# Stage borders of a gated attention and memory kernel: clears, stores and sweep steps issued elsewhere, a gate gradient as a column of other products

## The chip, the cores and the metric

The kernel runs on one core of one Trainium2 chip. The metric is the device time of one execution in microseconds (us), given as the median of several runs. TensorE (PE) does the matrix products, VectorE (DVE), ScalarE (ACT) and GpSimd (POOL) do the elementwise work, and SyncE (SP) issues transfers. SP, ACT and POOL each have a queue from which they issue DMAs. Each engine carries out its own instructions in the order of the program; what passes between engines is kept in order by semaphores.

## The reference

The reference computes a gated mix of two token mixers on the same input `x` (2048 tokens of 576), and the gradients of everything for a given `grad_out`:

```python
g = sigmoid((x * gate_w).sum(-1, keepdims=True))
a = A(x, A_wq, A_wk, A_wv, A_wo)      # 32 query heads of 18, one shared k and v, softmax over all 2048 keys
b = B(x, mem0, Wq, Wk, Wv, Wo, 32)    # 64 segments of 32 tokens, one after the other
out = g * a + (1 - g) * b
# B, for each segment: h = [mem (8 rows); segment (32 rows)], 32 heads of 128,
#   masked softmax attention within h, o = attention @ Wo, mem = o[:8], output rows = o[8:]
# returned: out, and the gradients of x, A_wq, A_wk, A_wv, A_wo, mem0, Wq, Wk, Wv, Wo, gate_w
```

In B the memory of a segment comes out of the segment before it, so its forward and its backward pass are chains of 64 steps. All tensors are bfloat16.

## The kernel before

The kernel is a sequence of stages, and each stage has its own tiles. Names of tiles carry a prefix by stage.

- **Preparation and projections** (0 to about 470 us).
- **Forward weave** (to 2123 us): the 64-step chain of B (`b_chain_fwd`, tiles `c_...`) woven with the first pass of A over blocks of 512 queries and 4 heads (`a_pass1`, tiles `a_...`). A block ends with `a_post`: the accumulator is copied to `a_acs` by ACT, transposed by PE (`c_x`), copied to `a_tk` by ACT, and POOL works out `a_ot`, `a_t`, `a_dq` and `a_qc`, which are stored by DMA to `otok_dram`, `dqtok_dram` and `qs_dram`. In the chain's last segment POOL also issues the stores of `c_oT`, `c_vmT`, `c_oh` and `memT_hist`, and makes `c_oh` from `c_oT` by a copy.
- **Bulk** (`b_bulk`, 2127 to 2762 us, tiles `x_...`): attention within segments for all tokens, 128 ticks in 32 chunks of four. Each tick goes through a written list of stages: transposes of q and dO (`x_tr`, copied to `x_qT` by DVE), scores, an exponential on ACT (`x_E`), a normalization on POOL (`x_P`), and so on. The memory rows of k and v lie in four tiles `x_kmB`, `x_vmB` (two each) that are cleared once and then have only their diagonal blocks loaded. SP loads chunks ahead in the order of `load(...)` calls.
- **Sweep and lead** (2763 to 2851 us): `a_pass2` is the second pass of A, a generator of sweep steps. One step is a score product (`b_S`), an exponential on ACT (`b_E`, 128x1024), the product `b_dP`, a product with the exponentials on DVE (`b_dS`) and accumulations (`b_acc`). A step reads a block of `qs_dram` (`b_QS`). `lead_dw` computes the gradients of two weights in units of 16 products into the PSUM tiles `r_pj` and `r_x` in turn; a unit's result is copied to `r_kvo` by ACT and stored by POOL. The generator yields after every 11 products.
- **Backward weave** (to 4369 us): the 64-step backward chain (`b_chain_bwd`, tiles `r_...`) woven with sweep steps. Its weights `WT` (12 pieces of 1152 KB) are loaded by SP, at points of the lead that `early_bwd` lists.
- **`b_post`** (to 4583 us, tiles `y_...`).
- **`b_dw`** (4583 to 5345 us): the gradients of the weights of B and `out`. For k = 0 to 15 the token rows of two blocks of 512 columns (`w_d`, 2 MB each, loaded one k ahead) are multiplied with the tokens (`w_h`) in groups; a group of k < 4 is two runs of 20 products of 128x288, the first 16 over tokens and the last 4 over memory rows. Sweep steps are issued between products, one whenever `WCOLS` columns have been computed. After the groups of each k, `gate` computes 128 rows of `out`: 10 products, then a chain on DVE (`o_diff`, `o_out`, `o_dg`, the gate's gradient `dz_all`).
- **`a_final`** (5345 to 5404 us, tiles `f_...`): transposes of `wq` into `f_wqT`, and for each of 16 token tiles five transposes (`f_ptr`), their copy (`f_T`), twelve products into `f_big`, a DVE step and a POOL step to `f_dx` and its store. Between them 80 small products `f_pk` give the gradients of wk and wv, `f_k`.

Products of all stages go through one helper, so PE's lines in the profile are L87 (products) and L92 (transposes), and evacuations by ACT and DVE are often L84 and L82. Stages up to `b_dw` are issued in the order in which the program writes them; in `a_final` a scheduler chooses the order.

Of the kernel before, what the change touches and what calls it, by code (L numbers as in the profile page):

```python
# [16 lines left out]
P = 128  # L17
# [23 lines left out]
WCOLS = 13824  # L41
# [10 lines left out]
class Kern:  # L52
# [295 lines left out]
    def b_chain_fwd(self, keep, sp, psum):  # L348
# [71 lines left out]
        for s in range(NSEG):  # L420
# [21 lines left out]
            def mT_store(w):  # L442
                nc.gpsimd.dma_start(self.mTd[w][s], mT[w][:].rearrange("p c u t -> p (c u) t"))
# [113 lines left out]
            nc.gpsimd.dma_start(self.oTm_dram[s // 16][:, s % 16, :], oT[:].rearrange("p u c q -> p (u c q)"))  # L557
# [10 lines left out]
            if s % 4 == 3:  # L568
                c0 = 8 * (s % 16 - 3)
                nc.gpsimd.dma_start(self.oh_dram[s // 16][:, :, c0:c0 + 32], oh[:].rearrange("p c u t -> p (c u) t"))  # L570
# [11 lines left out]
            else:  # L582
                nc.gpsimd.dma_start(self.memT_dram[:], hist[:])
# [87 lines left out]
    def early_bwd(self, i):  # L671
# [11 lines left out]
        for k in range(4):  # L683
# [4 lines left out]
            if i == PRE + 32 + k:  # L688
                self.load_WT(8 + k)

    def lead_dw(self, kvp, psum):
        nc = self.nc
        units = [(self.WT[w], o, kt, hf) for w, o in ((0, 2), (1, 5)) for kt in range(NKT) for hf in range(2)]
        n, out = 0, None
        for u, (t, o, kt, hf) in enumerate(units):
            rows = KT_ROWS[kt]
            pw = psum.tile([P, 512], F32, name=("r_pj", "r_x")[u % 2], bufs=1)
            for tt in range(self.NTT):
# [9 lines left out]
            def out(pw=pw, o=o, kt=kt, hf=hf, rows=rows):  # L708
                o16 = kvp.tile([P, 4, P], BF16, name="r_kvo", bufs=2)
                f = o16[0:rows].rearrange("p a b -> p (a b)")[:, 0:288]  # L710
                nc.scalar.copy(f, pw[0:rows, 0:288])
                nc.gpsimd.dma_start(self.outs[o][kt * P:kt * P + rows, 288 * hf:288 * hf + 288], f)
        out()
# [12 lines left out]
    def b_bulk(self, wp, lp, sp, psum):  # L726
# [4 lines left out]
        for t in mB["v"] + mB["k"]:  # L731
            nc.vector.memset(t[:], 0.0)
# [263 lines left out]
        for names in (deep, ("v", "vB", "kB")):  # L996
            load(1, names)
# [3 lines left out]
        for t in range(NG + 9):  # L1001
            for n, st in order:
# [445 lines left out]
    def b_dw(self, sp, wA, wB, wH, psum, sweep):  # L1448
# [30 lines left out]
        def groups(k, ts, ht):  # L1479
            if k < 4:  # L1480
                od = self.outs[10].rearrange("h e d -> (h e) d")
                for t, cs in ts:
                    for i in range(4):
                        o16 = sp.tile([P, D], BF16, name="w_o16b", bufs=3)
                        for hf in range(2):
                            acc = psum.tile([P, 512], F32, name="w_acc", bufs=3)
                            for it in range(n):
                                self.mm(acc[:, 0:288], lhsT=t[:, it, 128 * i:128 * i + 128],
                                        rhs=ht[:, it, 288 * hf:288 * hf + 288], start=(it == 0), stop=(it == n - 1))
                                weave(288)  # L1490
                            self.evac(o16[:, 288 * hf:288 * hf + 288], acc[:, 0:288])
# [27 lines left out]
        with self.tc.manual_schedule():  # L1519
# [7 lines left out]
            for _ in range(6):  # L1527
                next(sweep)
            for k in range(16):
# [13 lines left out]
                for _ in groups(k, ts, ht):  # L1543
# [4 lines left out]
            dz16 = sp.tile([P, NTT], BF16, name="w_dz", bufs=1)  # L1548
            nc.vector.tensor_copy(dz16[:], self.dz_all[:])
            pg = [psum.tile([P, 512], F32, name="w_acc", bufs=3) for _ in range(2)]  # L1550
            for tt in range(NTT):
                for hf in range(2):
                    self.mm(pg[hf][0:1, 0:288], lhsT=dz16[:, tt:tt + 1], rhs=ht[:, tt, 288 * hf:288 * hf + 288],
                            start=(tt == 0), stop=(tt == NTT - 1))
            dg16 = sp.tile([P, 2, 288], BF16, name="w_dg", bufs=1)
            for hf in range(2):
                nc.vector.tensor_copy(dg16[0:1, hf, :], pg[hf][0:1, 0:288])
            nc.sync.dma_start(self.outs[11][None, :], dg16[0:1].rearrange("p a b -> p (a b)"))
# [692 lines left out]
```

## Time and profile before

| | |
|---|---|
| median of 3 runs | 5409.53 us (5405.29, 5409.53, 5409.9) |
| profiled execution | 5406.08 us, of it span 5404.4 us |
| mean granted PE clock | 0.984 |
| busy: DVE, ACT, POOL | 66%, 61%, 41% of the span |
| DMA | 959.71 MB, mean 178 GB/s |

All views that are shown come from that one profiled execution. In a timeline, a row gives the start, the busy time, engine, line, operation, output and inputs and the number of instructions, and in brackets the engine's idle time before it and what ended it. A row of waits gives what an engine waited for: us in total, times, the longest. A row of stretches gives the busy time of PE, PE's weight load, DVE, ACT and POOL (instructions in brackets), the granted PE clock, the share of the DMA engines that is busy and GB/s.

### The profile page before, as it was taken

The numbers are of one execution on the slowest core, as the hardware profiler recorded it, in microseconds if no ns is written. First come the engines' busy times: TensorE is split into PE (matmuls) and PEld (weight loads), VectorE is DVE, ScalarE is ACT, GpSimd is POOL, SyncE is SP. The second block draws the span as 40 slices with busy tenths as digits, with TensorE's granted clock in tenths as the row PEclk, the third lists the DMA queues.
The fourth block names the chain that finished last, engine by engine and source line by source line (L and its number), as shares of the span: only waits on it lengthen the run. The fifth ranks groups of instructions, "written<-read, shape, count | busy, mean of one in ns | idle before, by whom it ended". The sixth has DMA issues, their size and how long they took to land. (4 is left out here: it accounts for less than half of the span.)

```text
span 5404.4 us, 221739 instructions
## 1 busy us (share of the span) xinstructions
PE 5156.3 (95%) x95713; PEld 2791.6 (52%) x95713; DVE 3568.7 (66%) x7079; ACT 3307.3 (61%) x4753; POOL 2189.9 (41%) x4199
## 2 busy tenths in 40 slices
PE   8999999999999998999988999999999999999998
PEld 6434444444444444666654555555555567754444
DVE  5337888888888887666657777878888841333322
ACT  4326778878888886555556777777777732222211
POOL 4004556565565655333323444444444421111213
PEclk9999999999999999999999999999999999999999
DMA  6645666676666555788885677888888778966653
GB/s 217 223 172 136 136 136 137 136 142 141 140 139 127 118 110 148 239 250 250 257 272 173 164 180 175 180 180 183 180 181 176 166 191 209 270 207 201 199 166 93
DMA packets 1065785, 959.71 MB, mean 178 GB/s; under 512 B 617506, under 2 KB 920363, under 8 KB 1054818
## 3 DMA queue, kind: packets, MB, share of 16 engines
q1 hardware_dynamic: 953762, 687.59, 52.8%
q0 software_dynamic: 102752, 248.05, 14.8%
q8 instruction: 749, 12.27, 1.0%
q10 hardware_dynamic: 8288, 9.87, 0.6%
q14 instruction: 234, 1.92, 0.1%
HBM read 518.41 MB, written 375.52 MB: 165 GB/s over the span
## 5 line engine op out<-in xcount | busy, mean ns | idle before, releaser
L1990 DVE TENSOR_TENSOR b_dS<-b_dP,b_E 128x512 bf16<-128x512 f32 x2048 | 1317.7, 685 | 584.6 <-PE b_dP L87 262.1
L1825 DVE TENSOR_TENSOR a_W<-a_dP,a_E 128x512 bf16<-128x512 f32 x2048 | 1314.5, 684 | 238.4 <-issue 108.5
L1939 ACT ACTIVATE b_E<-b_S 128x1024 bf16<-128x1024 f32 x1024 | 1049.5, 1025 | 626.8 <-PE b_dP L87 540.9
L1795 ACT ACTIVATE a_E<-a_S 128x1024 bf16<-128x1024 f32 x1024 | 1050.0, 1025 | 251.7 <-PE a_dP L87 166.9
L87 PE MATMUL r_pj<-WT,r_dT 128*32 128x288 bf16 x12288 | 488.9, 289 | 8.6 <-DMA WT<-st_WT 4.8
L87 PE MATMUL w_acc<-w_d,w_h 128*128 128x512 bf16 (+1 forms) x2400 | 484.1, 379 | 0.0
L87 PEld LDWEIGHTS <-b_QS 32*128 32x128 bf16 (+1 forms) x8192 | 229.2, 90 | 429.5 <-issue 376.8
L87 PE MATMUL b_S<-b_KV,b_QS 32*128 32x512 bf16 x2048 | 404.0, 387 | 36.7 <-ACT b_E L1939 24.5
L87 PE MATMUL a_S<-a_QD,l_KV 32*128 32x512 bf16 x2048 | 399.5, 384 | 38.4 <-ACT a_E L1795 36.1
L87 PE MATMUL a_acc<-a_W,l_WK 128*32 128x512 bf16 x4096 | 413.9, 390 | 1.3 <-issue 1.0
L87 PE MATMUL a_acc<-a_E,l_VK 128*32 128x512 bf16 x4096 | 403.7, 381 | 6.1 <-issue 1.1
L87 PE MATMUL b_dP<-b_KV,b_QS 32*128 32x512 bf16 x2048 | 404.5, 389 | 1.1 <-DVE r_xq L285 1.1
L87 PE MATMUL b_acc<-b_dS,b_QS 128*18 128x512 bf16 x2048 | 400.3, 385 | 0.4 <-DVE b_dS L1990 0.2
L87 PE MATMUL a_dP<-a_QD,l_KV 32*128 32x512 bf16 x2048 | 399.2, 386 | 0.0
L87 PE MATMUL b_acc<-b_E,b_QS 128*18 128x512 bf16 x2048 | 397.7, 385 | 0.6 <-issue 0.6
L87 PEld LDWEIGHTS <-r_dT 128*32 128x32 bf16 x12288 | 276.3, 96 | 163.6 <-issue 129.7
L87 PEld LDWEIGHTS <-w_h 128*128 128x128 bf16 (+1 forms) x2528 | 214.5, 100 | 248.8 <-issue 19.7
L87 PEld LDWEIGHTS <-hm 128*32 128x32 bf16 x7680 | 203.5, 97 | 197.7 <-issue 2.9
L938 POOL TENSOR_TENSOR x_prod<-x_dOT,x_oT 128x512 bf16<-128x512 bf16 x128 | 148.0, 1156 | 294.3 <-ACT x_oT L935 282.4
L87 PEld LDWEIGHTS <-l_KV 32*128 32x128 bf16 x4096 | 122.3, 91 | 249.3 <-issue 204.4
L87 PEld LDWEIGHTS <-l_WK 128*32 128x32 bf16 x4096 | 106.8, 93 | 221.7 <-issue 221.2
L87 PE MATMUL x_b<-WoN,x_oT 128*128 128x288 bf16 x1024 | 212.1, 291 | 0.8 <-issue 0.8
(465 smaller groups left out, 10120.6 us busy)
## 6 DMA issues: line engine op xcount, KB each, us to landing
b_QS<-qs_dram SPq DMA_DIRECT2D x233, 200.0 KB
dOx_dram<-p_tok SPq DMA_DIRECT2D x16, 1024.0 KB
c_vx<-vx_dram SPq DMA_DIRECT2D x64, 256.0 KB
krow_dram<-c_k POOLq DMA_DIRECT2D x64, 256.0 KB
qrow_dram<-c_q POOLq DMA_DIRECT2D x64, 256.0 KB
vrow_dram<-c_v POOLq DMA_DIRECT2D x64, 256.0 KB
x_q<-qx_dram SPq DMA_DIRECT2D x32, 512.0 KB
x_dO<-dOx_dram SPq DMA_DIRECT2D x32, 512.0 KB
```

The costliest lines, as they stand in the source:

```text
L87: return self.nc.tensor.matmul(out, lhsT, rhs, start=start, stop=stop, tile_position=tp, skip_group_check=True)
L938: nc.gpsimd.tensor_tensor(out=sc["prod", t][:], in0=sc["dOT", t][:], in1=oT[:], op=ALU.mult)
L1795: nc.scalar.activation(E_[n][:], S.pop(n)[:], ACT.Exp, scale=SCALEA)
L1825: nc.vector.tensor_tensor(out=W_[n][:, i, :], in0=dP[i][:], in1=E_[n][:, i, :], op=ALU.mult)
L1939: nc.scalar.activation(E_[n][:], S.pop(n)[:], ACT.Exp, scale=SCALEA)
L1990: nc.vector.tensor_tensor(out=D_[n][:, i, :], in0=dP[i][:], in1=E_[n][:, i, :], op=ALU.mult)
```

## The change

The change touches four borders between stages.

1. **Forward weave to bulk.** The stores of the last segment (`c_oT`, `c_vmT`, `c_oh`, `memT_hist`) and of the last `a_post` block (`a_ot`, `a_dq`, `a_qc`) are issued from ACT instead of POOL. Two of the four clears become ACT copies of zeros; the two others are done on DVE after tick 0, and the loads of these two tiles follow behind.
2. **Lead to backward weave.** The third group of `WT` loads is issued two rows earlier. A unit of `lead_dw` is evacuated and stored when it ends, instead of one step later.
3. **`b_post` to `b_dw`.** Six sweep steps ahead of `b_dw` are no longer issued there. Two are issued within the first group, between its 32 products over tokens and its 8 over memory rows; the others follow in the weave, whose `WCOLS` is 13312 instead of 13824.
4. **The end.** The gate of k = 15 is issued after group 3 of its k instead of after the last. The gradient of `gate_w` was 32 products of one column of `w_dz` with the tokens; it becomes a 37th column of the `f_pk` products, stored by five one-column stores. In `a_final` the last, 64-row piece of the contraction becomes a full 128-row tile that overlaps the one before, with zeros in the overlap of `f_wqT`; `f_T` is copied by one ACT copy of 128x640 instead of ACT and DVE; and the twelve products of a token tile have 288 columns each, instead of six of 512 and six of 64. The stores of `out_4` go from POOL to SP.

```diff
-WCOLS = 13824
+WCOLS = 13312
...
-                nc.gpsimd.dma_start(self.mTd[w][s], mT[w][:].rearrange("p c u t -> p (c u) t"))
+                (nc.scalar if last and w == "v" else nc.gpsimd).dma_start(self.mTd[w][s], mT[w][:].rearrange("p c u t -> p (c u) t"))
...
-            nc.gpsimd.dma_start(self.oTm_dram[s // 16][:, s % 16, :], oT[:].rearrange("p u c q -> p (u c q)"))
+            (nc.scalar if last else nc.gpsimd).dma_start(self.oTm_dram[s // 16][:, s % 16, :], oT[:].rearrange("p u c q -> p (u c q)"))
             nc.gpsimd.tensor_copy(oh[:, :, :, 8 * (s % 4):8 * (s % 4) + 8], oT[:].rearrange("p u c q -> p c u q"))
...
-                nc.gpsimd.dma_start(self.oh_dram[s // 16][:, :, c0:c0 + 32], oh[:].rearrange("p c u t -> p (c u) t"))
+                (nc.scalar if last else nc.gpsimd).dma_start(self.oh_dram[s // 16][:, :, c0:c0 + 32], oh[:].rearrange("p c u t -> p (c u) t"))
...
-                nc.gpsimd.dma_start(self.memT_dram[:], hist[:])
+                nc.scalar.dma_start(self.memT_dram[:], hist[:])
...
-            if i == PRE + 32 + k:
+            if i == PRE + 30 + k:
                 self.load_WT(8 + k)
...
-                if n % 11 == 0:
+                if n % 11 == 0 and tt < self.NTT - 1:
                     yield
-                    if out is not None:
-                        out()
-                        out = None
...
+            o16 = kvp.tile([P, 4, P], BF16, name="r_kvo", bufs=2)
+            f = o16[0:rows].rearrange("p a b -> p (a b)")[:, 0:288]
+            nc.scalar.copy(f, pw[0:rows, 0:288])
+            nc.gpsimd.dma_start(self.outs[o][kt * P:kt * P + rows, 288 * hf:288 * hf + 288], f)
+            if n % 11 == 0:
+                yield
...
-        for t in mB["v"] + mB["k"]:
-            nc.vector.memset(t[:], 0.0)
+        clear = lambda t: t[:].rearrange("p g i e -> p (g i) e")
+        for w in ("v", "k"):
+            nc.scalar.copy(clear(mB[w][0]), self.zeros[:].unsqueeze(1).to_broadcast([P, 16, P]))
...
-        for names in (deep, ("v", "vB", "kB")):
+        for names in (deep, ("v",)):
             load(1, names)
...
+            if t == 0:
+                for w in ("v", "k"):
+                    nc.vector.memset(mB[w][1][:], 0.0)
+                load(1, ("vB", "kB"))
...
+                        if k == 0 and cs.start == 0 and i == 0:
+                            for hf in range(2):
+                                part(hf, range(0, NTT))
+                            for _ in range(2):
+                                next(sweep)
+                            for hf in range(2):
+                                part(hf, range(NTT, n))
...
-            for _ in range(6):
-                next(sweep)
...
-                self.gate(k, gl, wo, sp, psum)
+                    if k == 15 and j == 3:
+                        self.gate(k, gl, wo, sp, psum)
+                if k < 15:
+                    self.gate(k, gl, wo, sp, psum)
...
-            pg = [psum.tile([P, 512], F32, name="w_acc", bufs=3) for _ in range(2)]
-            for tt in range(NTT):
-                for hf in range(2):
-                    self.mm(pg[hf][0:1, 0:288], lhsT=dz16[:, tt:tt + 1], rhs=ht[:, tt, 288 * hf:288 * hf + 288],
-                            start=(tt == 0), stop=(tt == NTT - 1))
...
-        dq_ = nc.gpsimd if late else nc.sync
+        dq_ = (nc.scalar if qb == self.T // 512 - 1 else nc.gpsimd) if late else nc.sync
...
+        nc.vector.memset(wqT[0:64, 4, :], 0.0)
...
+        nc.vector.tensor_copy(dkt[:, :, 36], self.dz16[:])
...
+            nc.scalar.copy(dqT[:], ptr[:])
+            pdx = psum.tile([P, 2, 512], F32, name="f_big", bufs=2)
+            pairs = [(dqT[:, kt, :], wqT[:, kt, :]) for kt in range(NKT)] + [(dkv[:, trows], wkvT[:])]
+            for i, (l, r) in enumerate(pairs):
+                for hf in range(2):
+                    self.mm(pdx[:, hf, 0:288], lhsT=l, rhs=r[:, 288 * hf:288 * hf + 288], start=(i == 0), stop=(i == len(pairs) - 1))
...
-            nc.gpsimd.dma_start(self.outs[4][cs, :], k16[0:drows, DA:36])
+            nc.sync.dma_start(self.outs[4][cs, :], k16[0:drows, DA:36])
+            nc.gpsimd.dma_start(self.outs[11][cs].rearrange("(p o) -> p o", o=1), k16[0:drows, 36:37])
```

More of the change, by code (lines that the diff above doesn't have):

```diff
@@ L1446, in b_post, with b_dw @@
                     load((t + 3) // 2, ("dq",))
-    def b_dw(self, sp, wA, wB, wH, psum, sweep):
+    def b_dw(self, keep, sp, wA, wB, wH, psum, sweep):
         nc = self.nc
@@ L1484, in groups, with part @@
                         o16 = sp.tile([P, D], BF16, name="w_o16b", bufs=3)
-                        for hf in range(2):
-                            acc = psum.tile([P, 512], F32, name="w_acc", bufs=3)
-                            for it in range(n):
-                                self.mm(acc[:, 0:288], lhsT=t[:, it, 128 * i:128 * i + 128],
+                        acc = {}
+                        def part(hf, its):
+                            if hf not in acc:
+                                acc[hf] = psum.tile([P, 512], F32, name="w_acc", bufs=3)
+                            for it in its:
+                                self.mm(acc[hf][:, 0:288], lhsT=t[:, it, 128 * i:128 * i + 128],
                                         rhs=ht[:, it, 288 * hf:288 * hf + 288], start=(it == 0), stop=(it == n - 1))
                                 weave(288)
-                            self.evac(o16[:, 288 * hf:288 * hf + 288], acc[:, 0:288])
+                            if its.stop == n:
+                                self.evac(o16[:, 288 * hf:288 * hf + 288], acc[hf][:, 0:288])
+                        if k == 0 and cs.start == 0 and i == 0:
[5 more added lines that the diff above has]
+                                part(hf, range(NTT, n))
+                        else:
+                            for hf in range(2):
+                                part(hf, range(0, n))
                         r0 = cs.start + i * 128
```

66 lines of the change are left out of this document (23 added, 43 removed).

## The prediction

> **What bounds the kernel now.** I read, in this order, the page's busy times, the waits of PE (TensorE) in the four border stretches that the diff touches, the timelines of these stretches, and their clock. The page first:
>
> ```profile
> PE 5156.3 (95%) x95713; PEld 2791.6 (52%) x95713; DVE 3568.7 (66%) x7079; ACT 3307.3 (61%) x4753; POOL 2189.9 (41%) x4199
> ```
>
> PE is the bound: of the span of 5404.4 us it is idle for only 248.1. An edit gains only where it takes away PE work or PE idle time, so each border is costed by what PE does there. Border 1, from the forward chain to the bulk stage (waits of PE, 2120 to 2150 us):
>
> ```profile
> PE x_tr L92 <- POOL x_P L915: 7.3, 2, 6.6
> PE x_tr L92 <- DVE x_qT L836: 4.2, 1, 4.2
> PE c_x L1862 <- ACT a_tk L84: 1.8, 1, 1.8
> ```
>
> DVE is late because four clears run on it, POOL because stores and the last a_post block stand ahead of x_P. POOL's timeline shows that queue, in which c_oh comes only after another a_post block's last store (issued 2128.25):
>
> ```profile
> 2128.83 0.55 POOL L557 DMA_DIRECT2D oTm_dram<-c_oT  x1
> 2129.38 0.42 POOL L558 COPY c_oh<-c_oT 128x256 bf16<-128x256 bf16 x1
> ...
> 2132.93 1.67 POOL L570 DMA_DIRECT2D oh_dram<-c_oh  x1 [1.15 <-issue]
> ...
> 2143.11 0.62 POOL L915 TENSOR_TENSOR x_P<-x_E,x_r 128x256 bf16<-128x256 bf16 x1
> ```
>
> Border 2, from the bulk to the backward chain (waits of PE, 2763 to 2900 us):
>
> ```profile
> PE r_pj L87 <- DMA WT<-st_WT: 4.8, 2, 3.0
> PE r_pj L87 <- ACT r_kvo L711: 4.4, 5, 2.3
> PE r_x L87 <- ACT r_kvo L711: 3.2, 4, 2.1
> ```
>
> Border 3, from b_post to b_dw: PE ends at 4583.42, then this timeline of PE:
>
> ```profile
> 4587.70 0.61 PE L87 MATMUL b_S<-b_KV,b_QS 32*128 32x512 bf16 x2 [4.28 <-DMA b_QS<-qs_dram]
> ...
> 4589.42 0.61 PE L87 MATMUL b_S<-b_KV,b_QS 32*128 32x512 bf16 x2 [1.11 <-ACT b_E L1939]
> ...
> 4599.22 8.33 PE L87 MATMUL w_acc<-w_h,w_d 128*128 128x288 bf16 x48
> ```
>
> Six sweep steps run alone there, each waiting for ACT's exponential. The clock by stretch (the figure of 0 to 1 is the granted share; the first two stretches belong to border 2):
>
> ```profile
> 2820.00:2830.00 10.00, 8.35 (x62) 4.42 (x62) 3.54 (x7) 4.05 (x6) 1.66 (x3) 0.83 0.76 252
> 2880.00:2890.00 10.00, 9.56 (x169) 3.66 (x165) 5.90 (x10) 6.33 (x10) 2.23 (x5) 0.65 0.17 40
> 4590.00:4600.00 10.00, 7.71 (x47) 2.08 (x44) 7.30 (x12) 6.04 (x6) 0.00 (x0) 0.50 1.13 285
> 4600.00:4610.00 10.00, 10.00 (x70) 6.75 (x69) 2.86 (x5) 1.71 (x4) 2.37 (x2) 0.80 1.08 358
> ```
>
> Idle PE also costs clock afterwards. Border 4, the last stage (timeline; the first two lines are the gate's products and the gate gradient):
>
> ```profile
> 5334.42 1.40 PE L87 MATMUL w_acc<-w_wo,o_T 128*128 128x288 bf16 x10
> ...
> 5338.61 6.99 PE L87 MATMUL w_acc<-w_h,w_dz 128*1 128x288 bf16 x32 [2.80 <-DVE w_dz L1549]
> ...
> 5361.55 0.09 PEld L87 LDWEIGHTS <-f_T 64*128 64x128 bf16 x1 [0.42 <-DVE f_T L82]
> ```
>
> **Border 1: +6 us.** Leaving: four DVE clears (0.91 each) and seven store issues on POOL (0.55 + 0.54 + 1.67 + 0.64 + 0.85 + 0.78 + 0.59 = 5.6). Coming: the same seven issues on ACT, two clears as ACT copies of 128x2048, two clears on DVE one tick later, and the loads of the second buffers behind the chunk loads on SP. If only this counted, PE's 4.23 and 6.59 would go: 10.8 gained. But ACT runs in order, and two waits now stand in its queue. The oh store waits for POOL's c_oh, which without the oTm issue ahead of it ends at 2128.83 + 0.42 = 2129.25. Behind it on ACT stands a_acs, which PE waits for and which ran at 2123.21; it moves to about 2129.9, and PE's first bulk transposes from 2126.59 to about 2132. The transposes that waited 4.23 come at about 2133.6 against 2132.20. Then otok, dqtok and qs wait on ACT for POOL's a_ot, a_dq, a_qc (last at about 2137.4, POOL being later by the shift and shorter by its issues), then the two copies (a 64x2048 copy on ACT takes 1.91 us; I take 1.85 for each), and only then the first x_E: about 2141.8 against 2134.72. PE's x_P transposes come at 2145.1 against 2143.79: +1.3. On SP the masked loads wait for the copies, and behind them stand the loads of chunk 1, now issued at about 2144 instead of 2132.6 to 2134.0. Four loads of 512 KB took about 8 us to land, PE wants the first at about 2146.5: +3.5. The longer idle stretch costs some clock (0.50 was granted in 2140 to 2150): +1. Sum +5.8, taken as +6. Ends: -10.8 (ACT never stands) and +10 (the loads 4 us later still).
>
> **Border 2: -11.2 us.** The evacuation of a lead_dw unit is issued at the unit's end instead of a step later. The r_kvo waits sum to 4.4 + 3.2 = 7.6; the last, 2.10 at 2853.28, follows the last unit, and stays: 5.5 gained. ACT stays half idle there, so nothing else is late. The third group of WT loads (1152 KB each) is issued two rows earlier, three in a row at 2856 to 2857 instead of 2856.2, 2861.05 and 2866.2 twice, the fourth at about 2862; the small r loads that they pass on SP are not needed sooner. From 195 GB/s in 2850 to 2860 and 383 in 2860 to 2870 the DMA has room for this; the 6.6 MB in flight land within 0.6 us of PE's wish, so of 4.8 I take 4.2. The clock loss after the two stalls (0.83 and 0.65 granted, 1.7 + 3.2 us) shrinks; as the 2.10 stays I count 1.5. Ends: -5.5 (WT still late) and -14.6.
>
> Here a rule differs from the row. The granted clock was 0.83 behind a single stall of 2.33 us. The Trainium skill, page "TensorE: Matmul & The Clock Gate", section "Part 1: The HAM clock gate", has the clock halved only after an idle window of about 3.4 us, so that such a stall alone should cost none; the row does not bear it out. By it the clock term of this border would be about 0.5 smaller, and border 1, where PE would stand for 6.7 us in one piece, about 1.7 us dearer (an estimate from that page): 2 us less gain in all.
>
> **Border 3: -9.5 us.** Before, 4583.42 to 4599.22 is 15.8, and the 48 products behind it took 8.33 against 5.99 at full clock: 2.4 more, 18.2 for six steps. After, 32 products (about 4.1, work that was to come anyway) cover b_QS's landing at 4587.7 but for 0.2. They need the first w_d load (2 MB, issued 4573.08, with 250 to 390 GB/s moved from 4574 to 4582): landed by about 4582, an estimate. Two steps then take 3.4, as before to 4591.14. The remaining 8 products wait for the oh transposes, whose issue ends on SP at 4589.17: about 1.5. Four steps woven in later cost 0.65 each (4607.48 to 4608.13), 2.6, and I leave 1 for clock. 0.2 + 3.4 + 1.5 + 2.6 + 1 = 8.7; 18.2 - 8.7 = 9.5. What is late next is the second w_d tile: issued 4589.49 with transposes to 4601.78, wanted at about 4609 instead of 4621. Ends: -4 (this tile 5 late) and -12. WCOLS only spaces the same steps closer; they end within k = 14 either way: nothing.
>
> **Border 4: -16.4 us.** The gate of k = 15 moves five groups up, so its DVE chain (o_diff to w_dz, 2.80 of PE idle) is hidden by some 20 us of products, and 32 products of 1x288 go: 2.80 + 6.92 = 9.7 of PE, with its store. Instead, 80 f_pk products have 37 columns for 36 (under 0.1). The last stage's inputs are wanted 9.7 earlier; their DMA burst (300 GB/s) ends at about 5322, before 5336. In the loop a pair of token tiles holds 24 f_big products, 3.87 us on the chain. As 24 of 288 columns at 0.125 (32 took 4.09) they take 3.0, and the DVE copy that PE's weight load waited for is gone: 0.87 in each of 8 pairs, 7.0. ACT copies 128x640 (0.72 by like rows) instead of 128x512 (0.588); f_pk products cover this in five pairs, and in the last three PE waits 0.5: 5.5 left. At the end POOL's last f_dx started 0.76 late and its store 0.48 late behind f_k issues, which now come earlier: 1.2. POOL carries 2 x 1.27 + 0.55 + up to 1.1 = 4.2 us a pair against about 4.5 of PE: not the bound, but near. Five stores of one column land well before the end: nothing. Ends: -10 (POOL the bound) and -18.
>
> **Sum.** 6 - 11.2 - 9.5 - 16.4 = -31.1. The profiled execution took 5406.1 (span 5404.4 and 1.7 around it); it would become 5375.0. It lies 3.4 under the median of 5409.5, so the forecast is 5378.4. About 0.2% (10.8 us) is what a measurement of this kernel can tell from no change.
>
> **Rivals.**
> 1. ACT does not stand at border 1, since c_oh comes in time. Against it: c_oh's place on POOL behind another block's stores. Border 1 is then -10.8: 5361.6.
> 2. The freed time goes into transfers: WT and the second w_d tile land late, and POOL bounds the last loop. All four near ends together: 10 - 5.5 - 4 - 10 = -9.5, that is 5400.0, no difference. For it: DMA shares over 1 from 4590 on; against it: PE waited for no w_d in all of b_dw.
> 3. Slower, by one mechanism: at border 1 the chunk loads leave SP 11 us late, and SP never catches up, so that every one of the bulk's later chunks meets its loads late. There are 32 chunks (x_q is loaded 32 times), so from (31.1 + 10.8)/30 = 1.4 us a chunk the kernel is slower by over 0.2%; at 2 us it is -31.1 + 60 = +29: 5438. For it: SP's queue is in order, and the loads lead by few chunks. Against it: loads are issued as buffers come free, and a chunk takes some 20 us (2127 to 2762 us holds the stage) against 11 of delay.
>
> **How the numbers follow.** The forecast has 0.73 (its own range 5368 to 5391), rival 1 0.11, rival 2 0.09, rival 3 0.07. Faster: 0.73 + 0.11 = 0.84; same: 0.09 with a little of its neighbours, 0.09; slower 0.07. The range takes half of rival 1 and some of the way to rival 2: 5363 to 5396.
>
> **What would show it.** Right: no r_kvo waits but the last and no WT wait; w_acc starting at about 4583.5, two lone sweep steps; no 1x288 products, f_wtr right behind w_acc; x_E on ACT at about 2141, a wait of 6 to 7 us ahead of c_x. Wrong: a c_x wait under 2 us (rival 1), waits of w_acc for w_d or of f_dx for POOL (rival 2), x_tr waits for x_q or x_k in later chunks (rival 3).

## The result, and the profile after

The changed kernel took 5423.34 us (median of 20 runs, 5408.27 to 5437.15), the kernel before 5409.23 us on the same chip (20 runs, 5392.67 to 5429.22). The ratio is 1.0026, with a 95% interval of 1.0017 to 1.0036: slower by 0.26%, where 5378.4 and faster had been forecast.

The profiled execution took 5412.21 us, its span is 5410.5. The page first, as for the kernel before:

```profile
PE 5118.4 (95%) x95504; PEld 2795.3 (52%) x95681; DVE 3563.6 (66%) x7061; ACT 3313.2 (61%) x4755; POOL 2185.2 (40%) x4192
```

PE's busy time can't be held against the one before as it stands: this trace has 95504 products for 95681 weight loads, the one before 95713 of each. The records of 177 products are missing, half of them of one group in the bulk (39 of the 128 products of `x_kmB` and `x_DT` are there). `e1_row` below, which is the change but for one part, has 95682 of each and 5132.2 us, 24.1 less than before. So work did go, and yet the span is 6.1 us longer. The stretches between fixed points of PE's timeline say where (us):

| stretch | before | after | change | forecast |
|---|---|---|---|---|
| border 1: end of the last `a_acc` product to the second `x_v` transposes | 31.46 | 36.56 | +5.1 | +6 |
| border 2, lead: third pair of `b_S` of the sweep to the first `r_x` on `WoT` | 85.99 | 81.34 | -4.7 | -5.5, and -1.5 of clock |
| border 2, `WT`: from there to the `b_S` behind 200 products on `WT`, which waits 0.58 for ACT | 38.88 | 38.79 | -0.1 | -4.2 |
| `b_dw` with border 3: start of the last copy to `y_dx` to the last `w_acc` product other than the gate gradient's | 752.35 | 756.7 | +4.4 | -9.5 |
| last stage: from there to the end of the span | 68.6 | 83.0 | +14.4 | -16.4 |

The changes sum to +19.1. The spans differ by 6.1, and the medians of 20 runs by 14.1, because stretches that nothing edited also differ from run to run (last section): these single executions are used to place a loss, and the ratios to say how large it is.

**Border 4** is where it went wrong. The first view below is of PE's waits from 5330 to 5411 us, the second of POOL's in the same stretch, the third is POOL's timeline there:

```profile
PE f_big L87 <- DVE f_dx L2074: 20.3, 4, 8.5
PE f_pk L87 <- DVE f_k L82: 7.1, 1, 7.1
PE f_big L87 <- ACT f_k L84: 2.5, 1, 2.5
PE f_big L87 <- ACT f_T L2067: 0.5, 3, 0.2
```

```profile
POOL f_dx L2077 <- DMA out_dram<-f_dx: 37.7, 11, 9.7
```

```profile
5339.37 0.55 POOL L2078 DMA_DIRECT2D out_dram<-f_dx  x1
5339.90 0.54 POOL L2091 DMA_DIRECT2D out_dram<-f_k  x1
...
5341.63 1.27 POOL L2077 TENSOR_TENSOR f_dx<-f_dx,w_d 128x576 bf16<-128x576 f32 x1 [1.18 <-DMA out_dram<-f_dx]
...
5351.63 1.27 POOL L2077 TENSOR_TENSOR f_dx<-f_dx,w_d 128x576 bf16<-128x576 f32 x1 [8.73 <-DMA out_dram<-f_dx]
...
5370.52 1.27 POOL L2077 TENSOR_TENSOR f_dx<-f_dx,w_d 128x576 bf16<-128x576 f32 x1 [9.68 <-DMA out_dram<-f_dx]
```

L2091 is the new store of one column of `f_k`. It costs POOL 0.54 us to issue, and from then on POOL's sum for a later token tile stands for up to 9.7 us: the tile's buffer is still being stored. The store of `f_dx` is the same as before, but it takes longer to land. DVE, which writes the tile first, stands behind POOL, and PE behind DVE: that is the 20.3 of the first view. The 7.1 and 2.5 have another way: `f_k` has two buffers as well, and its copies on DVE and ACT stood for the stores of an earlier `f_k` (which of its three stores, the view does not tell):

```profile
  DMA out_dram<-f_k: 24.1, 2
```

**Border 1** went as its working said. ACT's timeline has the oh store at 2124.49, and behind it `a_acs` with 8.56 us of waiting for POOL; the copies of zeros and the first `x_E` follow late. The second view is of PE's waits from 2110 to 2160:

```profile
2124.49 0.66 ACTq L570 DMA_DIRECT2D oh_dram<-c_oh  x1
2125.20 0.58 ACT L1842 COPY a_acs<-a_acc 128x512 f32<-128x512 f32 x1 [8.56 <-POOL c_PqB L275]
...
2134.27 1.90 ACT L729 COPY x_vmB<-zeros 128x2048 bf16<-128x2048 bf16 x1 [6.00 <-DMA otok_dram<-a_ot]
2136.07 1.89 ACT L729 COPY x_kmB<-zeros 128x2048 bf16<-128x2048 bf16 x1
2137.87 0.38 ACT L888 ACTIVATE x_E<-x_SD 128x256 bf16<-128x256 f32 x1
```

```profile
PE c_x L1871 <- ACT a_acs L1842: 7.4, 1, 7.4
PE x_SD L87 <- ACT x_E L888: 2.8, 1, 2.8
PE x_tr L92 <- DMA x_k<-kx_dram: 2.6, 1, 2.6
```

**Border 2.** PE's waits from 2763 to 2890 us have one short row for `r_kvo` instead of two that summed to 7.6, and the row for `WT` is longer than before, not shorter:

```profile
PE r_pj L87 <- DMA WT<-st_WT: 6.4, 2, 4.6
PE r_x L87 <- ACT r_kvo L706: 1.2, 1, 1.2
```

**Border 3.** Its timeline and waits of PE (4560 to 4640 us):

```profile
4571.44 4.08 PE L87 MATMUL w_acc<-w_h,w_d 128*128 128x288 bf16 x32 [0.73 <-ACT y_dx L1413]
...
4576.96 0.39 PE L87 MATMUL b_S<-b_KV,b_QS 32*128 32x512 bf16 x2 [1.12 <-ACT b_E L1948]
...
4583.84 3.39 PE L87 MATMUL w_acc<-w_h,w_d 128*128 128x288 bf16 x13 [4.30 <-DMA w_d<-oh_dram]
...
4597.09 0.61 PE L92 MATMUL z_pt<-identB,z_v 128*128 128x128 bf16 x4 [4.57 <-DVE z_v L623]
```

```profile
PE z_pt L92 <- DVE z_v L623: 4.6, 1, 4.6
PE w_acc L87 <- DMA w_d<-oh_dram: 4.3, 1, 4.3
PE b_S L87 <- ACT b_E L1948: 2.2, 2, 1.1
PE z_pt L92 <- POOL z_v L623: 1.1, 1, 1.1
```

The 32 products start as soon as the last `y_dx` is there, as forecast, and two sweep steps follow. But then PE stands for the memory rows (`w_d` from `oh_dram`, 4.3) and for the memory tokens (`z_v`, 5.7), neither of which it waited for before. The granted clock (in the eighth place of the stretches) is hardly better than before, when the three stretches from 4580 to 4610 had 0.84, 0.50 and 0.80:

```profile
4580.00:4590.00 10.00, 6.16 (x39) 3.86 (x40) 0.72 (x2) 2.34 (x3) 0.55 (x1) 0.66 1.12 263
4590.00:4600.00 10.00, 4.29 (x33) 2.99 (x32) 2.25 (x4) 0.92 (x2) 2.90 (x2) 0.73 1.07 356
4600.00:4610.00 10.00, 10.00 (x71) 6.52 (x70) 2.44 (x4) 1.92 (x3) 0.54 (x1) 0.76 1.22 276
```

SP issues these two transfers as late as before. Here are its rows for the memory rows of the first tile and for the memory tokens, first before, then after:

```profile
4573.50 15.67 SPq L1472 DMA_TRANSPOSE w_d<-oh_dram  x4
4601.88 0.99 SPq L612 DMA_DIRECT2D z_src<-dTm_dram  x2
```

```profile
4560.79 15.61 SPq L1473 DMA_TRANSPOSE w_d<-oh_dram  x4
4590.94 0.99 SPq L612 DMA_DIRECT2D z_src<-dTm_dram  x2
```

Counted from the start of the last copy to `y_dx` (4583.46 and 4570.75), the last of the four transposes is issued by 5.7 us in both, and the tokens at 18.4 us before and 20.2 after.

### The profile page after: what moved, and what is told of

Read it like the earlier page. It is cut to its first block, busy times and chain, and to the rows that moved or that the text cites. A ratio compares the mean times of both kernels' runs of the same rounds, so it can differ in the third digit from the quotient of the medians.

```text
span 5410.5 us, 221493 instructions
## 1 busy us (share of the span) xinstructions
PE 5118.4 (95%) x95504; PEld 2795.3 (52%) x95681; DVE 3563.6 (66%) x7061; ACT 3313.2 (61%) x4755; POOL 2185.2 (40%) x4192
## 5 line engine op out<-in xcount | busy, mean ns | idle before, releaser
L87 PE MATMUL r_pj<-WT,r_dT 128*32 128x288 bf16 x12288 | 487.4, 289 | 11.1 <-DMA WT<-st_WT 6.4
L87 PE MATMUL a_S<-a_QD,l_KV 32*128 32x512 bf16 x2048 | 398.9, 384 | 37.0 <-ACT a_E L1804 35.6
```

The source lines that it names most:

```text
L87: return self.nc.tensor.matmul(out, lhsT, rhs, start=start, stop=stop, tile_position=tp, skip_group_check=True)
```

## Experiments

Theory: the five one-column stores delay the stores beside them, and nearly the whole loss of border 4 is theirs. The rivals: POOL's queue is too full, whatever it issues; or the 288-column products and the 640-column copy bring the waits. Borders 1 to 3 are then taken apart one by one. "The stretch of a border" is that of the table above.

### The column stored as two rows

In `e1_row` the five pieces of the column are gathered in a tile of 128 by 5, which PE transposes; two stores of rows replace the five of one column. All else is as in the changed kernel.

```diff
-            nc.gpsimd.dma_start(self.outs[11][cs].rearrange("(p o) -> p o", o=1), k16[0:drows, 36:37])
+            nc.vector.tensor_copy(g5[0:drows, kt:kt + 1], k16[0:drows, 36:37])
+        self.tr(pt[0:NKT, 0:P], g5[:], P)
+        nc.vector.tensor_copy(gr[0:NKT, :], pt[0:NKT, 0:P])
+        nc.sync.dma_start(self.outs[11][0:512].rearrange("(k p) -> k p", p=P), gr[0:4, :])
+        nc.sync.dma_start(self.outs[11][512:D].rearrange("(k p) -> k p", k=1), gr[4:5, 0:64])
```

> The changed kernel with the gate gradient's column collected over the five groups in one 128x5 tile, transposed by PE and stored as rows of 256 bytes by two SP stores, instead of five stores of 2 bytes per partition. Last stage counted from the last product of b_dw to the end of the span: 68.6 us before, 83.0 after. Theory 1 (the 2-byte stores hold the transfers behind them, and PE waits for f_dx's buffers): last stage 52 to 56 us, no wait of f_big for f_dx over 1 us, time about 30 us under the changed kernel, 5390 to 5396. Theory 2 (the wider products, the single ACT copy or POOL are what slows the loop): last stage 78 us or more, time within 5 us of the changed kernel.

5381.73 us (6 runs) beside 5401.97 (9 runs) of the kernel before: 0.9963, interval 0.9945 to 0.9981. The last stage takes 45.6 us instead of 83.0, less than the 52 to 56 expected. PE's waits of the last stage are down to one row for the copy of `f_T`, and the landing of `f_dx` (us from issue; first the changed kernel, then `e1_row`) is short again:

```profile
PE f_big L87 <- ACT f_T L2067: 1.6, 6, 0.6
```

```profile
DMA to landing us min/median/max: 2.0/7.1/12.1
```

```profile
DMA to landing us min/median/max: 2.0/2.0/3.0
```

So the products and the copy are not the cause of the loss, and with this one part mended the change is faster than the kernel before.

### The same five stores added to the kernel before

`e2_before_cols` is the kernel before, with five stores of one column of `f_k` into a scratch of 640 by 1.

```diff
+        self.gcol_dram = dram.tile([NKT * P, 1], BF16, name="gcol_dram")
...
             nc.gpsimd.dma_start(self.outs[4][cs, :], k16[0:drows, DA:36])
+            nc.gpsimd.dma_start(self.gcol_dram[cs, :], k16[0:drows, 35:36])
```

> The kernel before with nothing changed but five more stores on POOL: one column (2 bytes per partition, 128 rows next to each other) of f_k to a scratch tensor in DRAM, each behind the store of out_4. It measures the disputed cost by itself. Theory 1: the last stage goes from 68.6 to 85 to 100 us, with waits of POOL f_dx for f_dx's stores of 5 us or more, time 15 to 30 us over before. Theory 2: last stage 68 to 72 us, time as before.

5446.17 us (4 runs): 1.0076, interval 1.0056 to 1.0095, slower than the kernel before by 44 us at the medians. The last stage takes 115.2 us instead of 68.6. Both are more than expected. POOL's row of the last stage:

```profile
POOL f_dx L2075 <- DMA out_dram<-f_dx: 47.9, 3, 17.8
```

The same wait as in the changed kernel, without any other edit of it. The five stores are enough.

### The stores on ACT's queue

`e3_act` is the changed kernel with the five stores issued by ACT.

```diff
-            nc.gpsimd.dma_start(self.outs[11][cs].rearrange("(p o) -> p o", o=1), k16[0:drows, 36:37])
+            nc.scalar.dma_start(self.outs[11][cs].rearrange("(p o) -> p o", o=1), k16[0:drows, 36:37])
```

> The changed kernel with the five one-column stores issued from ACT instead of POOL. If the cost sits in POOL's own queue (the f_dx and f_k stores that stand behind them there): last stage 52 to 60 us. If it sits in the writes themselves or in the engines that all queues share: last stage 75 us or more, with f_dx's stores from POOL and SP still late. Theory 2: 78 us or more.

5437.1 us (one run), last stage 100.2. The wait is still POOL's, for stores that POOL and SP issued, though the column is now in another queue:

```profile
POOL f_dx L2077 <- DMA out_dram<-f_dx: 57.5, 7, 18.9
```

It is not POOL's queue that is full; the writes hold up what other queues issue. The Trainium skill, page "DMA: Bandwidth & Descriptors", section "Issuing engines are not separate DMA queues", says that starting DMAs from several engines saves only the time to start them; this row agrees.

### The same writes, 64 bytes apart

`e4_spaced` is `e1_row` with five stores of one column again, on POOL, into a scratch whose rows lie 64 bytes apart. The number of 2-byte writes is that of the changed kernel.

```diff
+        self.gcol_dram = dram.tile([NKT * P, 32], BF16, name="gcol_dram")
...
             nc.vector.tensor_copy(g5[0:drows, kt:kt + 1], k16[0:drows, 36:37])
+            nc.gpsimd.dma_start(self.gcol_dram[cs, 0:1], k16[0:drows, 36:37])
```

> As the kernel that stores the gate gradient as rows, plus the five one-column stores on POOL again, now to a scratch tensor whose rows are 64 bytes apart instead of 2. If writes next to each other in the same small stretch of DRAM hold each other up: last stage 52 to 60 us. If the number of 2-byte writes counts, wherever they go: last stage 75 us or more.

5380.9 us (one run), last stage 47.0 against 45.6 of `e1_row`. PE waits for the copy of `f_T` 1.2 us and for the gathered row 0.4, and no store of `f_dx` is waited for:

```profile
PE f_big L87 <- ACT f_T L2068: 1.2, 5, 0.6
PE f_big L87 <- DVE f_gr L2099: 0.4, 1, 0.4
```

It is not that the writes are many or of two bytes. It is that they are neighbours: 128 of them fall into 256 bytes of memory. Distances between 2 and 64 bytes were not tried.

### Border 3 taken back

`e5_no_border3` is `e1_row` with the six sweep steps ahead of `b_dw` and the old `WCOLS`. The split of the first group into 32 and 8 products stays.

```diff
-WCOLS = 13312
+WCOLS = 13824
...
-                            for _ in range(2):
-                                next(sweep)
...
+            for _ in range(6):
+                next(sweep)
```

> The kernel that stores the gate gradient as rows, with border 3 undone (six sweep steps ahead of b_dw, WCOLS 13824). Read from the trace: time from y_dx's copy to the store of group 32 of the first weight gradient (206.2 and 207.3 us in two traces with border 3 as before; 205.6, 207.3, 209.3 and 209.5 in four with it changed) and to the start of the last stage (751.3 and 752.4; 752.8 to 756.7). Theory A (the arrival of the first w_d tiles, oh rows and z_src sets the pace; the moved steps only change where PE waits): 206 to 208 and 751 to 753, that is no gain from border 3. Theory B (border 3 gains as forecast, and something else in b_dw takes it back): 5 us or more later than with it.

5356.42 us (one run; the kernel before took 5400.25 in one run on this chip). `b_dw` takes 752.2 against 752.9 of `e1_row`. Over all kernels, one execution each, it took 752.35, 751.3, 752.2, 751.0 and 750.4 with border 3 as before (mean 751.4), and 756.7, 752.9, 756.6, 754.6, 756.1 and 757.6 as changed (mean 755.7); the two sets do not overlap. So border 3 costs some 4 us and gains nothing. Where it goes is seen in the time from the start of the copy to `y_dx` to the store of a group of `w_acc` (us):

| group | 1 | 2 | 3 | 16 | 32 |
|---|---|---|---|---|---|
| kernel before | 24.2 | 29.8 | 35.6 | 114.2 | 207.3 |
| changed | 15.9 | 28.4 | 37.6 | 116.2 | 209.5 |
| `e1_row` | 13.6 | 25.9 | 33.8 | 112.3 | 205.6 |
| `e5_no_border3` | 24.1 | 29.8 | 35.5 | 114.1 | 207.3 |

The first group is 8 to 11 us earlier, as forecast, and by the third all or nearly all of it is given back, though about four sweep steps fewer (0.65 each, 2.6 in all) have been done by then.

### Six steps inside the first group

```diff
-                            for _ in range(2):
+                            for _ in range(6):
                                 next(sweep)
```

> As the kernel that stores the gate gradient as rows, but with all six steps, not two, issued within the first group between its 32 and its 8 products. Theory A: the four more steps fall into the wait for the transfers, the wait for oh rows is gone, group 3 is stored at most 2 us later than in that kernel (33.8 us after y_dx), and group 32 comes 2 to 5 us earlier (201 to 204). Theory B (PE's own work sets the pace there): the steps cost what they cost before, 1.8 us each, group 3 comes 5 us or more later and group 32 at 207 or later.

`e6_six` (on `e1_row`): 5361.28 us, one run. Group 3 comes at 37.2, between the two expectations, and group 32 at 209.1, where the second had it (207 or later). PE's waits for `w_d` and `z_v` are gone, and those of the steps are back. The longest of them is of the fourth step, for which ACT stood 6.13 us behind a `b_QS` load that it could issue only at 4573.60:

```profile
PE b_S L87 <- ACT b_E L1948: 9.3, 6, 5.8
```

```profile
4573.60 0.33 ACTq L1934 DMA_DIRECT2D b_QS<-qs_dram  x1
4573.98 1.02 ACT L1948 ACTIVATE b_E<-b_S 128x1024 bf16<-128x1024 f32 x1 [6.13 <-DMA w_d<-oh_dram]
```

So six steps there do cover both transfers, at no gain, since a wait came that the six steps ahead of `b_dw` did not have. In the changed kernel the same exponential stood 5.79. The profile names the memory rows' landing as what held this load. What ties the two together was not tried, and what six steps would cost without that wait is open.

### The memory tokens later

In `e7_z_late` (on `e1_row`) the generator that reads and transposes the memory tokens (`z_v`, `z_pt`) starts four groups later.

```diff
-                    next(mem, None)
+                    if k > 0 or j > 3:
+                        next(mem, None)
```

> As the kernel that stores the gate gradient as rows, but the transposes of mem_tok (z_pt, behind z_src and z_v) start only after the fourth group of k = 0 instead of the first. If the waits for z_v (4.3 + 1.1 us and the clock they cost) are a loss of their own: group 3 is stored 4 to 7 us earlier (27 to 30 us after y_dx) and group 32 at 199 to 202. If the transfers set the pace: PE waits for the second w_d tile instead, and group 32 changes by under 2 us.

5372.25 us, one run. Groups 2, 3 and 16 come at 22.8, 28.4 and 105.4, which is 7 to 9 us ahead of the kernel before and 3 to 7 ahead of `e1_row`; PE has no wait for `z_v` there any more. But group 17 comes at 117.1, and group 32 at 205.1, hardly ahead of `e1_row`'s 205.6. PE's timeline shows the one new wait, for the same tokens a stage further on:

```profile
4680.20 1.14 PE L87 MATMUL w_acc<-w_h,w_d 128*128 128x288 bf16 x8 [2.76 <-ACT z_tk L84]
```

The memory tokens were put off past the point where the products of the next k need them. Moving a wait moved it.

### Border 1: the oh store back on POOL

```diff
-                (nc.scalar if last else nc.gpsimd).dma_start(self.oh_dram[s // 16][:, :, c0:c0 + 32], oh[:].rearrange("p c u t -> p (c u) t"))
+                nc.gpsimd.dma_start(self.oh_dram[s // 16][:, :, c0:c0 + 32], oh[:].rearrange("p c u t -> p (c u) t"))
```

> As the kernel that stores the gate gradient as rows, but the oh store of the last segment is issued from POOL again. If ACT stood behind c_oh (the step of the forecast for border 1): the wait of c_x for a_acs falls from 7.4 us to under 1.5, and the stretch from the last a_acc to the first transposes of x_v in the bulk (27.4 us before, 33.1 after) falls to 24 to 28. If ACT stood behind another wait: the wait of c_x stays over 5 us.

`e8_oh_pool` (on `e1_row`): 5369.26 us, one run. PE's wait ahead of `c_x` falls from 7.4 to 0.7 us, so the oh store in ACT's queue was its cause. The stretch of the border is still 36.0 (36.5 in `e1_row`; to the expectation's mark, the first `x_v` transpose, 32.5 and not 24 to 28), since the wait comes back at the exponentials:

```profile
PE x_SD L87 <- ACT x_E L888: 9.3, 1, 9.3
...
PE c_x L1871 <- ACT a_acs L1842: 0.7, 1, 0.7
```

ACT's timeline shows what is now ahead of `x_E`: the stores of `a_ot`, `a_dq` and `a_qc`, for which ACT waits on POOL, and the two copies behind them:

```profile
2124.23 0.40 ACTq L1902 DMA_DIRECT2D otok_dram<-a_ot  x1
...
2126.71 1.90 ACT L729 COPY x_vmB<-zeros 128x2048 bf16<-128x2048 bf16 x1 [12.42 <-DMA otok_dram<-a_ot]
...
2130.31 0.38 ACT L888 ACTIVATE x_E<-x_SD 128x256 bf16<-128x256 f32 x1
```

One thing more differs, 3200 us later: from POOL's last store of `f_dx` to the end of the span it is 10.4 us here and 5.2 in `e1_row`. Of the fourteen kernels, the six in which POOL issues the last segment's oh store have 10.4 to 11.1 us there (15.6 in `e2_before_cols`, with its column stores), and the eight in which ACT issues it 5.2 to 5.6. Why is not shown, but the edit that costs PE its 7.4 us at border 1 goes with some 5 us less at the end.

### One `WT` load earlier

```diff
-            if i == 30 + 2 * k:
+            if i == 29 + 2 * k:
                 self.load_WT(4 + k)
```

> As the kernel that stores the gate gradient as rows, but the second group of WT loads is issued one lead step earlier, so that its last load stands on SP ahead of r_k and r_dx, which hold SP from 2838.7 to 2847.8 in the trace of the changed kernel. If SP's order is why the WT waits did not shrink: the sum of r_pj's waits for WT falls from 6.3 us to under 3.5, and the stretch from r_x<-WoT to the b_S behind the WT products from 28.4 to 24 to 26 us. If the transfers' rate sets it: waits and stretch within 1 us of 6.3 and 28.4.

`e9_wt` (on `e1_row`): 5350.84 us, one run. PE's wait for `WT` falls from 4.5 to 1.2, as the first expectation had it, but the expectation's stretch, which ends 10 us ahead of that of the table, only from 28.4 to 27.2, not to 24 to 26; the table's is 35.3 instead of 38.45. A wait for the small `r_dx` load, which the pieces now pass on SP, takes the place of the other:

```profile
PE r_pj L87 <- DMA r_dx<-dmx_dram: 3.2, 1, 3.2
...
PE r_pj L87 <- DMA WT<-st_WT: 1.2, 1, 1.2
```

With the same edit the table's stretch is 36.4 in `e10_best` and 38.9 in `e12_best_z` (next section), where `r_dx` is waited for 6.2 and 3.5 us; without it, it is 37.0 to 38.8 in the nine kernels with the new lead. So it is not settled that the earlier load gains anything.

### Taken together

`e11_no_border13` is `e1_row` with borders 1 and 3 as before. `e10_best` is `e1_row` with border 3 as before, the earlier `WT` load, and a border 1 in which only the stores of `oTm`, `vmT` and `memT` go to ACT; the oh store and those of `a_post` stay on POOL, and the clears on DVE (two ahead, two after tick 0). Of its border 1 and its `WT`:

```diff
-            nc.scalar.copy(clear(mB[w][0]), self.zeros[:].unsqueeze(1).to_broadcast([P, 16, P]))
+            nc.vector.memset(mB[w][0][:], 0.0)
...
-        dq_ = (nc.scalar if qb == self.T // 512 - 1 else nc.gpsimd) if late else nc.sync
+        dq_ = nc.gpsimd if late else nc.sync
```

`e12_best_z` is `e10_best` with border 3 as changed, and the memory tokens two groups later:

```diff
-                    next(mem, None)
+                    if k > 0 or j > 1:
+                        next(mem, None)
```

> As the kernel that stores the gate gradient as rows, with borders 1 and 3 undone, so that the lead's evacuation, the WT order and the last stage remain. If borders 1 and 3 cost what the traces say (5 us and 0 to 4 us): 5 to 9 us under that kernel, 20 to 35 us under before (ratio 0.9935 to 0.9965). If they gain as the sum of the forecast had it for border 3 (9.5): 4 us or more over that kernel.

> What the runs so far point to: the kernel that stores the gate gradient as rows, with border 3 undone, the WT load one step earlier, and at border 1 only the stores of oTm, vmT and memT on ACT, oh and the last a_post block's stores on POOL, and all four clears on DVE, two ahead and two behind tick 0. Border 1, from the last a_acc to the second of the x_v transposes (31.5 us before, 36.5 with the change): 27 to 30, if the copies of zeros and the stores in front of x_E were what ACT lost; still 34 or more if the clears' place on DVE and the late loads were. Time: 25 to 40 us under before (ratio 0.993 to 0.995).

> As the best version so far, but with border 3 changed as in the change and the transposes of mem_tok starting two groups later. If the wait for z_v was what border 3 lost: group 16 is stored 106 to 110 us after y_dx (114.1 with border 3 undone), and b_dw, from y_dx to the last stage, takes 746 to 749 us instead of 752. If the loss only moves again: 751 or more. Time: 0 to 6 us under that version.

| kernel | median, runs | ratio to before (5390.24, 22 runs) | interval | border 1 | `b_dw` | last stage |
|---|---|---|---|---|---|---|
| `e11_no_border13` | 5368.64, 10 | 0.9966 | 0.9948 to 0.9985 | 31.46 | 750.4 | 50.8 |
| `e10_best` | 5359.54, 8 | 0.9941 | 0.9920 to 0.9962 | 29.8 | 751.0 | 50.7 |
| `e12_best_z` | 5359.25, 9 | 0.9943 | 0.9928 to 0.9959 | 29.6 | 751.0 | 51.6 |

`e10_best` and `e12_best_z` beat the kernel before by about 0.6% and the changed kernel by more. Their intervals overlap that of `e1_row` (0.9945 to 0.9981), so the medians alone don't say that mending borders 1 to 3 adds anything; the stretches do for border 1 (29.8 and 29.6 instead of 36.5). `e11_no_border13` can't be told from `e1_row` at all: it has 5 us less at border 1 and 2 to 4 less in `b_dw`, but, with the oh store on POOL again, 5 more in the last stage (50.8 instead of 45.6). `e10_best` and `e12_best_z` pay the same 5. `e12_best_z` missed its expectation for `b_dw` (746 to 749). Its groups are early (18.7, 25.2, 30.8, 109.4, 203.7), 3.6 us ahead of the kernel before at group 32, of which up to 2.6 are sweep steps not yet done; at the end nothing is left. The wait that remains early on is the oh rows':

```profile
PE w_acc L87 <- DMA w_d<-oh_dram: 7.1, 1, 7.1
PE b_S L87 <- ACT b_E L1948: 2.2, 2, 1.1
```

## Why the prediction was wrong

**Border 1 (+6): right.** It cost 5.1. The mechanism is the one worked out: the oh store ahead of `a_acs` on ACT (7.4 us of PE, forecast 6 to 7), copies of 1.90 and 1.89 (forecast 1.85). The first `x_E` comes 19.5 us after the end of `a_acc`, 11.55 before; so late an `x_E` was in the working (18.6), and PE's wait for `x_SD` (2.8) is its row. The late chunk loads were in it as well: PE waits 1.5 for `x_q` and 2.6 for `x_k`, 4.1 where 3.5 had been taken. What it lacks is the end of the span: `e8_oh_pool` and the split of the fourteen kernels give the same edit some 5 us back there, so that over the whole kernel border 1 may cost nothing. Rival 1 is refuted by the 7.4, and rival 3 as well: from 2165 to 2755 us PE waits for no load of a chunk at all. Rival 2, no difference because the freed time goes into transfers, is the nearest to what came: its signs, waits of `w_acc` for `w_d` and of `f_dx`, are there, though POOL did not stand for work of its own, and the loss went beyond its 5400.

After the wait of 7.4 us the granted clock was 0.50 from 2120 to 2150. Before, three of the five stretches of 5 us from 2125 to 2150 had 0.50 too, with shorter waits. The clock-gate rule of the Trainium skill (page "TensorE: Matmul & The Clock Gate", section "Part 1: The HAM clock gate") was weighed in the prediction: by it, an estimate, this border would have been 1.7 dearer. The border came out at 5.1, nearer to the 6 without that surcharge, but a single execution of each kernel can't decide on 1.7.

**Lead (-5.5, with the clock -7): right.** The stretch took 86.0 before and 83.8 in `e2_before_cols`, which has the old lead, and 81.3 in the changed kernel and 77.1 to 79.7 in all others. The last wait for `r_kvo` stayed, as forecast (1.2 for 2.10). (Of the clock term, 10 us at 0.65 are a loss of 3.5, not 3.2; nothing rests on it.)

**`WT` (-4.2): wrong.** The step that failed is "the 6.6 MB in flight land within 0.6 us of PE's wish". PE, freed of the lead's stalls, wants `WT` 5.3 us earlier as well (first `r_x` on `WoT` at 2847.98 instead of 2853.28). It waits ahead of the last two of its twelve runs of 16 products on `WT`. The last two pieces were issued 12.8 and 5.6 us earlier (2853.40 and 2861.18 instead of 2866.22 and 2866.79), but those two runs could start only 6.5 and 4.9 us earlier (2868.05 and 2873.31). The DMA had no room to catch up: from 2860 to 2870 it moved 385 GB/s, 383 before, with a share over 1 both times. And SP took longer over the small loads between the two pieces: 2.46 and 2.00 us to issue `r_vmT` and `r_vxT`, 0.33 and 0.49 before. The prediction counted a supply that got earlier and a demand that stayed. That the small r loads "are not needed sooner" fails too where pieces pass them earlier still: in `e9_wt`, `e10_best` and `e12_best_z` PE waits for `r_dx`.

**Border 3 (-9.5): wrong, it costs about 4.** The first group did come 8.3 us earlier. The step that failed is "18.2 for six steps": those 18.2 us were taken as time in which nothing but the steps held PE, all of it to be gained. The rows after show two transfers behind them, the oh rows (4.3) and `z_v` (5.7 with POOL's part), which are issued from points that did not move, and which the six steps had covered: neither is waited for before, nor with all six steps in the first group. The working named a next wait, the second `w_d` tile, and priced the oh transposes at 1.5, from the end of their issue; PE's wait for them ended 7.4 us after it, and `z_v` was not on the list. The clock term was not saved either (0.66, 0.73 and 0.76). What stays open: `e7_z_late` and `e12_best_z` removed the `z_v` wait and were still no faster at the end of `b_dw`, so those two waits place the loss in the first groups, but not the last 2 to 4 us of it.

**Border 4 (-16.4): the gain was sized right, and the cost left out.** Without the column stores the time from the last `w_acc` product other than the gate gradient's to the last store of `f_dx` is 17.1 us shorter (57.5 before, 40.4 in `e1_row`, 40.1 in `e10_best`), against 16.4 in the sum. The step that failed is "Five stores of one column land well before the end: nothing". They were judged by when they themselves land. What counts is what they do to the buffers that turn over every few us, the two of `f_dx` and the two of `f_k` (20.3 and 9.6 of PE's waits): the landing of the `f_dx` stores went from a median of 2.0 to 7.1 us, and the last stage from 45.6 (rows) to 83.0 (columns), a cost of 37 us in these executions; the two ratios, 1.0026 and 0.9963, differ by 0.0063, or 34 us of 5409. `e2_before_cols`, `e3_act` and `e4_spaced` show it to be these writes, in both queues that were tried, and only as neighbours. That the stores slow down one another because they go to the same few bytes fits this and was not tried further. The Trainium skill, page "DMA: Bandwidth & Descriptors", section "Specifications", says that transfers of less than 512 bytes make the engines read, modify and write. That alone doesn't explain the rows: the spaced writes are just as small and cost at most 1.4 us of the last stage.

With the terms as measured (border 1 +5, border 2 -5 to -8, border 3 +4, border 4 -17, and -6 from the last store of `f_dx` to the end of the span) the sum is -19 to -22; `e1_row`, which has all of these and rows for the column, measured -20 at the medians, with an interval of -30 to -10.

## What to carry to other kernels

A column of 2-byte values should not be stored one element per partition into neighbouring bytes: turn it into a row first (a transpose of 128x5 cost nothing that could be seen), and judge any odd store by the stores that share its time, not by its own landing. Before idle time or lone steps ahead of a stage are counted as a gain, list every transfer that this stage waits for and ask from which point each is issued; the ones that don't move with the edit are what the time goes to. When an earlier edit lets an engine arrive sooner, its loads need as much again to be early.

## What the runs showed of the hardware

- 128 neighbouring 2-byte writes to device memory cost the issuing engine 0.54 us, and held other stores up to 10 us in the changed kernel and, issued from another queue than these, up to 19 us in `e3_act` (the longest waits of POOL for `f_dx`); the same writes 64 bytes apart cost at most 1.4 us of the last stage.
- The time from the last store of `f_dx` on POOL to the end of the span was 5.6 us in the changed kernel and 5.2 in `e1_row`, but 11.1 in the kernel before and 10.6 in `e10_best`. In all fourteen kernels it goes with the engine, ACT or POOL, that issues the oh store of the last segment, some 3200 us earlier. No run tells why; it is part of the last-stage figures above.
- Stretches that hardly an edit touches differ widely over the fourteen profiled executions, which come from several chips: the last `a_acc` product ended between 2110.5 and 2126.3 us, the bulk stage took 595 to 616 us, the backward weave with `b_post` 1718 to 1739. Single runs of the kernel before differ by 37 us on one chip. Edits of 2 to 5 us were therefore read from the stretch between two fixed points, and only sums over 0.2% from the medians.
